# New hand-written instruction orders for the last six chunks of an attention and MoE kernel

## The chip, the cores and the metric

The kernel runs on one core of a Trainium2 chip. A time is device microseconds (us) of one execution; the time shown for a kernel is the median of several executions. A profile is one execution more, recorded by the hardware profiler, with its own time. The engines of the core are PE (TensorE: matmuls, and PEld, its weight loads), DVE (VectorE), ACT (ScalarE), POOL (GpSimd) and SP, which here issues nearly all DMAs. Each engine runs its own instructions strictly in order and waits for others at semaphores.

## The reference

For 8 batches and 8 heads, 512 local tokens and 32 global tokens with head size 64 attend to each other; what comes out is normed and put through a gated two-layer network.

```python
k_all = concat([k_g, k_l]); v_all = concat([v_g, v_l])
out_g = softmax(scale * q_g @ k_all.T) @ v_all                  # global rows see everything
mask  = abs(i - j) <= 32                                        # local rows: a band, and the globals
out_l = softmax(concat([scale * q_l @ k_g.T, where(mask, scale * q_l @ k_l.T, -1e9)])) @ v_all
x  = concat([out_g, out_l]) as (8 * 544, 512)
xn = x / sqrt(mean(x * x) + 1e-6) * rms_g
y  = (silu(xn @ w_gate) * (xn @ w_val)) @ w_out                 # 512 -> 1536 -> 512
```

## The kernel before, in words

The 4352 rows are worked in nine chunks. Chunks 0 to 7 hold the 512 local rows of one batch each, chunk 8 the 256 global rows of all batches. While PE works on the network of chunk c, attention for chunks c+1 and c+2 is woven in between.

The network's products are f16 matmuls. Each operand is split into a high and a low half, so that a product takes three matmuls. From chunk 2 on the first layer is written with seven block products instead of eight (`moe_pair`), and from chunk 3 on the second layer too (`moe_out`). The work of a chunk is a list of units. In chunks 3 to 7 units 0 to 41 are the first layer: steps P0 to P41, of 12 matmuls each (in chunk 8 there are 48 steps of 6). The second layer's steps are O0 to O41, of 6 matmuls each (3 in chunk 8). A matmul comes with one weight load, so P stands for 24 instructions of PE and O for 12. What other engines do with the result of unit k is called Rk (PSUM read and combined), tk (tanh, gating and splitting of an earlier group), nk (norm of the next chunk) and wk (a weight fetch that SP issues, 24 for the first layer and 11 for the second).

Attention units run beside it. A local unit (`local_halves`, four heads' worth: half a batch) has the steps L and V (loads), S (scores on PE, four PSUM banks), M and N (minimum, on DVE), E and F (exponentials, on ACT), D (division, on DVE and then on ACT or POOL), T (32 by 32 transposes on DVE), A and B (two parts of the products with V, on PE), X and Y (results out of PSUM). A global unit (`global_unit`) has GL, GV, GS, GM, GN, GT, GA, GD and GX; GS, GT, GA and GX are PE's. These products are f32, and the trace shows each of their matmuls as two: S is 128 matmuls and weight loads, A and B are 80 each, GS 32, GA 80, and the two halves of GT are 5 transposes each, GX one. Chunks 3 to 5 hold two local units and one global unit, chunk 6 one and one, chunk 7 two global units, chunk 8 none. The name `A/2+1.0` is step A of unit 2 of the chunk one further on, first piece; a step is cut into pieces where the engine changes.

The order of all this is not left to a scheduler. A planner runs once, and every engine call is stored under the name of its step (`write`, L1850). Then, for a chunk that has an entry in `ORDERS`, the calls are issued in the order of that list:

```python
    orders = {c: names.split() for c, names in ORDERS.items()}
    for c, plan in plans.items():
        for name in orders.get(c, plan):
            for call in plan.pop(name) if c in orders else plan[name]:
                call()
```

So a list sets the order of the instructions on each engine and of the DMAs on SP's queue. It neither adds nor drops an instruction. Tiles come from pools with a fixed number of buffers: fetched weights and most of the first layer's f32 results share the 12 buffers of the pool `wf`, attention on PE has 4 PSUM banks (`pa`), and the products have 4 (`po` twice, `pg`, `pv`). Whoever writes a new tile waits until the tile that had the buffer is done with. The numbers of lines in the profile are those of the call that issues (L1870 for nearly everything from chunk 1 on), so instructions are told apart by their tiles: `pq` is P, `pr` is O, `s` is S, `a` is A and B, `et` is what T writes, `wt` and `wu` are fetched weights.

Of the kernel before, what the change touches and what calls it, by code (L numbers as in the profile page):

```python
# [126 lines left out]
t18.0 t16.2 V/2+1.0 P16.0 S/2+1.0 P17.0 R15.1 P18.0 R16.0 M3/2+1.0 R17.0 E3/2+1.0 M2/2+1.0 N3/2+1.0
w13.0 t12.0 w15.0 E2/2+1.0 P19.0 R18.0 M0/2+1.0 N2/2+1.0 M1/2+1.0 E1/2+1.0 P20.0 R19.0 R20.0 w24.0
N1/2+1.0 t21.0 R20.2 F3/2+1.0 t19.1 D3/2+1.0 R20.1 t21.1 t22.0 t17.2 F2/2+1.0 P21.0 R21.0 P22.0
R22.1 R22.0 t19.0 t23.1 t22.1 t23.0 F1/2+1.0 D1/2+1.0 t17.3 D3/2+1.1 GA/1+1.0 t24.0 w17.0 t23.2  # L130
t24.3 w18.0 P23.0 R23.0 GN/1+1.2 P24.0 N0/2+1.0 R24.0 t24.1 T3/2+1.0 P25.0 P26.0 R25.0 R26.0 P27.0
R27.2 w20.0 E0/2+1.0 P28.0 GD/1+1.0 GX/1+1.0 F0/2+1.0 w22.0 R27.1 t28.1 R27.0 D0/2+1.0 D2/2+1.0
# [6 lines left out]
O0.0 t42.1 R41.2 E1/0+2.0 w38.0 N3/0+2.0 R41.0 t42.0 O3.0 t33.0 O1.0 O4.0 O7.0 t43.1 t43.0 t40.1
t44.0 t44.4 E0/0+2.0 t44.1 O2.0 O5.0 O8.0 t44.2 M2/0+2.0 n44.0 n44.1 w44.0 n44.2 O6.0 O11.0 N2/0+2.0  # L140
E2/0+2.0 F2/0+2.0 t45.1 t44.3 t45.0 w40.0 O9.0 O12.0 O15.0 N0/0+2.0 O10.0 t40.0 N1/0+2.0 w46.0 O14.0
w52.0 F1/0+2.0 M3/0+2.0 E3/0+2.0 t46.0 O17.0 R50.0 n44.3 n44.4 n44.5 D1/0+2.0 D1/0+2.1 n44.6 n44.7
O13.0 F0/0+2.0 t33.1 t46.1 R49.0 O16.0 O24.0 O25.0 O26.0 O27.0 O28.0 w50.0 n44.8 n44.9 w55.0 n44.10
n44.11 n44.12 D2/0+2.0 D2/0+2.1 n44.13 n46.0 w48.0 n47.1 R50.1 O29.0 F3/0+2.0 D0/0+2.0 R56.0 O18.0
O19.0 D0/0+2.1 n46.1 n48.1 n47.0 n48.0 w53.0 n49.0 O36.0 R50.2 T1/0+2.0 O37.0 O38.0 O39.0 O40.0
t45.2 D3/0+2.0 n54.1 T2/0+2.0 O41.0 R62.0 O20.0 O21.0 O22.0 w60.0 GL/1+2.0 T0/0+2.0 n53.2 n52.1
O23.0 D3/0+2.1 T3/0+2.0 A/0+2.0 n54.0 n51.1 n52.0 n49.1 n55.0 n53.0 B/0+2.0 X/0+2.1 w59.0 n49.2
n53.1 R53.0 O30.0 O31.0 O32.0 O33.0 w57.0 n50.0 n51.0 n55.1 n56.0 w62.0 X/0+2.0 X/0+2.2 O34.0 O35.0
R59.0 R62.1 R59.1
# [19 lines left out]
O1.0 t44.4 t38.1 t37.1 t39.0 O4.0 O7.0 w36.0 O10.0 O9.0 Y/2+1.3 w38.0 O12.0 t44.0 t44.2 t44.3 n42.0
O8.0 w40.0 t44.1 t45.0 n42.1 O11.0 t46.0 w44.0 t40.0 t45.1 O13.0 O14.0 t38.3 O15.0 R49.0 n44.0 n44.1  # L170
w48.0 n44.2 n44.3 n44.4 n44.5 n44.6 n44.7 O16.0 R50.1 O17.0 O18.0 O19.0 n44.8 w46.0 w50.0 w60.0
t46.1 R50.0 R50.2 O20.0 n44.9 O21.0 O22.0 O23.0 t40.1 O24.0 O25.0 O26.0 n44.10 n44.11 n44.12 n44.13
n46.0 t45.2 O27.0 O28.0 O29.0 n47.1 w52.0 O30.0 O31.0 R56.0 O36.0 w55.0 n47.0 n46.1 O37.0 O38.0
n48.0 n48.1 n53.2 n49.0 n49.1 n50.0 n51.0 w57.0 n49.2 w53.0 R53.0 w62.0 O39.0 O40.0 O41.0 R62.0
# [6 lines left out]
w4.0 w6.0 R10.0 w8.0 GS/0+1.0 GM/0+1.0 P12.0 R12.0 R13.1 t10.1 t14.1 w10.0 P13.0 R13.0 R13.2 t14.0
P14.0 R14.0 P15.0 w18.0 t11.0 P16.0 R15.1 GN/0+1.0 R15.0 R16.0 t15.1 w11.0 P17.0 t12.0 GM/0+1.1
P19.0 P18.0 GN/0+1.1 R18.0 R17.0 P20.0 t15.0 t16.0 t12.1 t16.2 GV/0+1.0 R20.2 GT/0+1.0 P21.0 P28.0
w13.0 GT/0+1.1 R19.0 R20.0 t21.0 R20.1 t21.1 t22.1 t10.2 GT/0+1.2 P23.0 t16.1 GT/0+1.3 GA/0+1.0
t17.2 t17.3 t17.0 t17.1 w17.0 P22.0 R21.0 P24.0 GN/0+1.2 w15.0 t10.3 w20.0 t22.0 t23.2 t23.0
GL/1+1.0 t24.0 R22.1 t24.3 w22.0 R22.0 t18.0 t24.1 GD/0+1.0 P25.0 R25.0 t19.1 R23.0 t23.1 t25.0
R24.0 P26.0 R26.0 R27.0 w25.0 t28.0 P29.0 R28.0 R29.1 t26.0 t26.1 P27.0 R27.2 t29.0 P30.0 R29.0
R30.0 P31.0 GS/1+1.0 GM/1+1.0 GN/1+1.0 P32.0 w27.0 R32.0 R31.0 GM/1+1.1 P33.0 R33.0 P35.0 R27.1
t28.1 t29.1 t30.1 R34.0 t35.0 R34.1 t35.1 w24.0 w29.0 t30.2 P36.0 t19.0 R35.0 R36.0 GV/1+1.0 P37.0
t24.2 t31.2 R36.1 w31.0 R37.0 P34.0 R34.2 t36.0 P38.0 R38.0 t30.0 GN/1+1.1 t31.0 t31.1 w32.0  # L190
GT/1+1.2 P39.0 R39.0 t31.3 t36.1 t37.0 t38.0 t37.1 GT/1+1.0 GT/1+1.1 P40.0 w34.0 GX/0+1.0 P41.0
R41.2 GT/1+1.3 GA/1+1.0 t32.0 t33.0 t37.2 t38.2 R40.0 R41.1 t38.3 GN/1+1.2 GD/1+1.0 t42.1 R41.0
# [1916 lines left out]
```

## Time and profile before

Three executions took 919.73, 917.34 and 916.6 us: a median of 917.34 us. The profiled execution took 915.97 us, of which the span from its first to its last instruction is 914.2 us.

| | us | share of the span |
|---|---|---|
| PE busy | 873.6 | 96% |
| PEld busy | 670.3 | 73% |
| DVE busy | 722.5 | 79% |
| ACT busy | 556.1 | 61% |
| POOL busy | 274.2 | 30% |

| stretch (PE's first product of the chunk to that of the next), us | length | PE busy | DVE busy |
|---|---|---|---|
| chunk 3, 384.27 to 482.25 | 97.98 | 96.12 | 80.18 |
| chunk 4, 482.25 to 583.60 | 101.35 | 97.58 | 78.75 |
| chunk 5, 583.60 to 681.86 | 98.26 | 96.24 | 78.74 |
| chunk 6, 681.86 to 774.27 | 92.41 | 91.63 | 73.16 |
| chunk 7, 774.27 to 865.28 | 91.01 | 90.66 | 64.70 |
| chunk 8, 865.28 to 910.64 | 45.36 | 45.36 | 23.31 |

The first table is the profile page's own sum. The second comes from the view that gives each engine's busy time in chosen stretches. Length less PE busy is the time in which PE did nothing; the mean granted TensorE clock of the whole run was 0.983 of full speed.

### The profile page before, as it was taken

What the parts mean: (1) busy time and instruction counts of PE and PEld (TensorE: products, weight loads), DVE (VectorE), ACT (ScalarE), POOL (GpSimd) and SP (SyncE); (2) the same over time, 40 slices, a digit from 0 to 9 for tenths busy, and PEclk for the clock granted to TensorE, in tenths of its full rate; (3) what the DMA queues carried; (4) which work ended last, traced back from release to release, by engine and by line L of the source; (5) the groups of instructions that cost most, each with busy time, mean ns of one, the idle gap of its engine ahead of it and who ended that gap; (6) DMA issues with size and microseconds to landing.
All of it is one profiled execution on the core that took longest, in us unless ns stands there. A gap on an engine that the chain in (4) does not pass through costs nothing.

```text
span 914.2 us, 27773 instructions
## 1 busy us (share of the span) xinstructions
PE 873.6 (96%) x11430; PEld 670.3 (73%) x11430; DVE 722.5 (79%) x1831; ACT 556.1 (61%) x1341; POOL 274.2 (30%) x244
## 2 busy tenths in 40 slices
...
GB/s 345 404 287 103 210 52 174 173 276 285 100 192 249 255 228 236 186 296 213 262 259 262 199 290 257 200 235 251 252 253 240 206 213 219 254 267 220 263 232 177
DMA packets 101006, 212.03 MB, mean 232 GB/s; under 512 B 8080, under 2 KB 34448, under 8 KB 100880
## 3 DMA queue, kind: packets, MB, share of 16 engines
...
q8 instruction: 89, 1.46, 0.6%
q10 hardware_dynamic: 432, 0.33, 0.1%
...
## 4 chain that ended last, share of the span: by engine, by line
PE 81%; DVE 4%; ACT 3%; issue 2%; DVEq 0%; ACTq 0%
PE pq L1870 33%; PE pr L1870 17%; PE p L1870 10%; PE po L1870 7%; PE po L1735 3%; PE a L1870 3%; PE s L1870 3%; PE ga L1870 1%; PE gt L1870 1%; PE gs L1870 1%; ACT e L1870 1%; DVE s L1870 1%; ACT s L1870 0%; PE s L629 0%; PE t L673 0%
## 5 line engine op out<-in xcount | busy, mean ns | idle before, releaser
L1870 PEld LDWEIGHTS <-wt 128*128 128x128 f16 x3312 | 321.5, 98 | 44.7 <-issue 6.3
L1870 PE MATMUL pq<-xh,wt 128*128 128x256 f16 x1152 | 203.1, 273 | 0.8 <-ACT s L1870 0.2
L1870 PE MATMUL pq<-xl,wt 128*128 128x256 f16 x576 | 157.0, 273 | 0.0
L1870 PE MATMUL pq<-ht,wt 128*128 128x256 f16 x1296 | 155.2, 273 | 0.0
L1870 ACT ACTIVATE e<-e,sm 128x128 f32<-128x128 f32 x288 | 104.3, 390 | 12.6 <-DVE sm L1870 12.6
L1870 PE MATMUL pr<-wu,hs 128*128 128x256 f16 x792 | 93.0, 275 | 3.3 <-issue 3.3
L1870 POOL TENSOR_TENSOR hu<-v,hu 128x256 f16<-128x256 f32 (+1 forms) x60 | 56.2, 949 | 127.4 <-ACT hu L1870 114.6
L1870 POOL TENSOR_TENSOR e<-e,sm 128x512 f32<-128x512 f32 x24 | 29.6, 1243 | 215.7 <-DVE sm L1870 209.5
L1870 POOL TENSOR_TENSOR hs<-u,hs 128x512 f16<-128x512 f32 x50 | 59.0, 1194 | 104.7 <-ACT hs L1870 101.5
L1870 PEld LDWEIGHTS <-hs 128*128 128x128 f16 x792 | 77.8, 99 | 13.5 <-issue 3.6
L1870 ACT COPY s<-pq 128x512 f32<-128x512 f32 x72 | 41.7, 580 | 58.1 <-PE pq L1870 30.8
L1870 PE MATMUL pr<-wu,hu 128*128 128x256 f16 x594 | 69.4, 273 | 0.0
L1870 ACT ACTIVATE t<-u,half_inv 128x512 f32<-128x512 f32 x72 | 49.5, 715 | 31.9 <-DVE u L1870 30.9
L1870 DVE TENSOR_TENSOR v<-pq,s 128x512 f32<-128x512 f32 x72 | 49.3, 685 | 20.2 <-PE pq L1870 17.4
L1870 PE MATMUL po<-wo,h 128*128 128x512 f16 x288 | 65.2, 386 | 0.0
L1870 DVE TENSOR_TENSOR s<-pq,s 128x512 f32<-128x512 f32 x66 | 44.9, 686 | 24.9 <-PE pq L1870 10.6
L1870 PEld LDWEIGHTS <-hu 128*128 128x128 f16 x594 | 58.1, 98 | 6.7
L1592 PE MATMUL p<-xh,wf 128*128 128x512 f16 x192 | 58.8, 379 | 3.5 <-DVE t L1704 1.6
L1870 DVE SCALAR_TENSOR_TENSOR t<-t,u 128x512 f32<-128x512 f32 x72 | 54.0, 759 | 6.5 <-ACT t L1870 6.5
L1870 PE MATMUL p<-xh,wf 128*128 128x512 f16 x192 | 58.6, 379 | 0.0
L1592 PEld LDWEIGHTS <-wf 128*128 128x128 f16 x288 | 27.7, 98 | 37.5 <-issue 3.5
L1870 PEld LDWEIGHTS <-h 128*128 128x128 f16 x288 | 28.4, 100 | 34.0 <-issue 2.5
...
## 6 DMA issues: line engine op xcount, KB each, us to landing
wt<-wd SPq DMA_DIRECT2D x120, 512.0 KB, 5.2
wu<-wb SPq DMA_DIRECT2D x36, 512.0 KB, 4.6
wr<-in_w_in_dram SPq DMA_DIRECT2D x24, 512.0 KB, 9.0
wu<-wa SPq DMA_DIRECT2D x24, 512.0 KB, 4.5
...
```

What stands on the lines that cost most here:

```text
L1592: nc.tensor.matmul(ps[:, :n], rows[:, a, o : o + P], ch[z][k][:, :n], start=(k == 0 and i == 0), stop=(k == NK - 1 and i == 2),)
L1735: nc.tensor.matmul(po[j], ch["h", f][:, a, j * P : (j + 1) * P], wo[f][:, z, :], start=(f == 0 and q == 0), stop=(f == NF - 1 and q == 2),)
L1870: return lambda *a, **k: write(self.engine, lambda: call(*a, **k))
```

## The change

Chunks 3, 4 and 5 shared one list before. Now each of the chunks 3 to 8 has a list of its own, and all six are new. Each new list holds exactly the names that the old one of its chunk held. Chunks 0, 1 and 2, the planner, the tiles and all the instructions are as before. The lines below are those of the lists that hold A and B, the beginning of the wait for them, and the fetches of chunk 6; the remaining lines are other orders of the same names.

```diff
 _ORDER_3 = """
...
-P34.0 R34.2 R34.0 R34.1 P36.0 R36.0 L/0+2.0 A/2+1.0 t35.1 t36.1 t30.0 t35.0 t36.0 t30.1 t31.3 P35.0
-R35.0 t31.2 t37.0 t31.0 t26.0 t37.2 w34.0 R36.1 B/2+1.0 w31.0 X/2+1.0 X/2+1.1 X/2+1.2 P37.0 t38.0
...
-O23.0 D3/0+2.1 T3/0+2.0 A/0+2.0 n54.0 n51.1 n52.0 n49.1 n55.0 n53.0 B/0+2.0 X/0+2.1 w59.0 n49.2
-n53.1 R53.0 O30.0 O31.0 O32.0 O33.0 w57.0 n50.0 n51.0 n55.1 n56.0 w62.0 X/0+2.0 X/0+2.2 O34.0 O35.0
...
+GD/1+1.0 R31.0 P34.0 P37.0 D1/2+1.1 t31.2 T1/2+1.0 t32.0 t33.1 w36.0 R34.0 t35.0 w34.0 R34.2 w48.0
+R35.0 P38.0 T3/2+1.0 A/2+1.0 B/2+1.0 R36.1 R36.0 R34.1 R37.0 P39.0 w32.0 P40.0 t35.1 t36.1 t36.0
...
+A/0+2.0 n54.1 B/0+2.0 R53.0 n53.2 R56.0 O36.0 O37.0 n48.0 t45.2 n48.1 n49.0 w57.0 R59.0 R59.1 n49.1
...
+_ORDER_4 = """
...
+P33.0 R33.0 R34.1 P34.0 P36.0 T1/2+1.0 R34.2 R34.0 t35.0 R35.0 A/2+1.0 B/2+1.0 Y/2+1.0 P38.0 R36.0
...
+n55.1 w62.0 n51.0 n52.0 O35.0 R59.0 w59.0 n52.1 n53.1 n56.0 A/0+2.0 B/0+2.0 X/0+2.0 X/0+2.1 X/0+2.2
+R59.1 n53.2 n54.0
+_ORDER_5 = """
...
+GV/1+1.0 R15.1 P16.0 R16.0 S/2+1.0 M0/2+1.0 M1/2+1.0 t16.1 E0/2+1.0 E1/2+1.0 P18.0 N1/2+1.0 t10.2
...
+D0/2+1.1 T0/2+1.0 w25.0 t29.0 t24.3 D3/2+1.1 T3/2+1.0 t29.1 R32.0 P33.0 R33.0 t30.0 R34.0 R31.0
+A/2+1.0 B/2+1.0 t31.0 Y/2+1.0 X/2+1.0 t26.1 X/2+1.1 X/2+1.2 X/2+1.3 R34.1 t35.0 t31.1 t30.1 t32.0
...
+T2/0+2.0 w62.0 R62.0 n49.2 n51.1 n52.0 w60.0 w57.0 R62.1 A/0+2.0 B/0+2.0 R53.0 R59.0 X/0+2.0 X/0+2.1
...
 _ORDER_6 = """
-P1.0 P0.0 R0.0 Y/0+1.1 R1.1 Y/0+1.0 P2.0 R1.0 R2.0 GS/1+1.0 w3.0 GM/1+1.0 GM/1+1.1 GN/1+1.0 P4.0
...
-P8.0 R8.1 R8.0 GT/1+1.0 GT/1+1.2 GT/1+1.3 GT/1+1.1 t7.1 t8.1 t9.2 w4.0 P9.0 P11.0 w13.0 t9.0 P14.0
...
-F0/2+1.0 D0/2+1.0 w18.0 P24.0 R20.1 t21.1 t22.0 P23.0 w17.0 E1/2+1.0 R22.0 R23.0 P25.0 E2/2+1.0
...
-A/2+1.0 B/2+1.0 R36.0 R34.0 t35.0 R35.0 P38.0 t32.0 t33.0 t36.0 t33.1 X/2+1.1 X/2+1.0 X/2+1.2 P37.0
...
+M1/2+1.0 N0/2+1.0 w11.0 R20.1 P22.0 R22.0 F3/2+1.0 E1/2+1.0 t21.0 w13.0 P23.0 R23.0 P21.0 w17.0
...
+D2/2+1.1 t32.0 T1/2+1.0 R33.0 P36.0 T3/2+1.0 T2/2+1.0 t33.0 R35.0 P37.0 R34.2 R36.1 A/2+1.0 B/2+1.0
...
-ORDERS = {1: _ORDER_1, 2: _ORDER_2, 3: _ORDER_3, 4: _ORDER_3, 5: _ORDER_3, 6: _ORDER_6, 7: _ORDER_7, 8: _ORDER_8}
+ORDERS = {1: _ORDER_1, 2: _ORDER_2, 3: _ORDER_3, 4: _ORDER_4, 5: _ORDER_5, 6: _ORDER_6, 7: _ORDER_7, 8: _ORDER_8}
```

On PE alone, the old and the new lists read as follows around the runs that matter below. GS, GT, S, GA and GX are left out of the P lists where they are not between the steps named.

| chunk | before | after |
|---|---|---|
| 3 | P34 P36 A/2 P35 B/2 P37 ... O20 to O23 A/0 B/0 O30 to O35 | P34 P37 P38 A/2 B/2 P39 ... O27 O28 O29 A/0 B/0 O36 to O41 |
| 4 | as chunk 3 | P34 P36 A/2 B/2 P38 ... O30 to O35 A/0 B/0, the chunk's end |
| 5 | as chunk 3 | P32 P33 A/2 B/2 P34 ... O36 to O41 A/0 B/0, the chunk's end |
| 6 | P36 P34 A/2 B/2 P38 P37 P39 P40 P41, then O | P36 P37 A/2 B/2 P39 P38 P40, O2 O5 O1 GX P41, then O |
| SP's fetches in 6 | w3 w1 w4 w13 w6 w8 w11 w10 w15 | w4 w3 w1 w10 w8 w6 w15 w11 w13 |

## Rows read from the trace of the kernel before

**Rows 1.** Busy time by stretch: length, PE, PEld, DVE, ACT, POOL (xinstructions), clock, DMA, GB/s.
```profile
384.27:910.64 526.37, 517.59 (x6965) 454.86 (x6958) 398.86 (x969) 301.36 (x722) 169.93 (x164) 1.00 0.75 240
```

**Rows 2.** Waits of PE in that stretch: us in total, times, longest.
```profile
PE a L1870 <- issue: 4.0, 3, 1.7
...
PE a L1870 <- DVE et L1870: 0.7, 2, 0.3
PE pq L1870 <- ACT s L1870: 0.2, 1, 0.2
```

**Rows 3.** Timeline of PE: start, us, what, count, idle before it and its releaser.
```profile
443.27 0.33 PE L1870 MATMUL a<-et,v 32*64 32x32 f32 x11 [1.71 <-issue]
...
572.47 2.38 PE L1870 MATMUL a<-et,v 32*64 32x256 f32 x160
574.78 1.27 PE L1870 MATMUL pr<-wu,hs 128*128 128x256 f16 x10
579.33 4.43 PE L1870 MATMUL pr<-wu,hs 128*128 128x256 f16 x26 [3.29 <-issue]
...
677.28 0.70 PE L1870 MATMUL a<-et,v 32*64 32x64 f32 x42 [1.54 <-issue]
...
739.45 0.68 PE L1870 MATMUL a<-et,v 32*64 32x64 f32 x40 [0.74 <-issue]
```

**Rows 4.** Busy time by stretch, from one such idle time to the next.
```profile
443.27:579.33 136.06, 132.29 (x2044) 116.56 (x2044) 110.83 (x294) 92.45 (x249) 46.56 (x43) 1.00 0.78 253
579.33:677.28 97.95, 95.93 (x1405) 83.65 (x1405) 77.12 (x202) 64.69 (x170) 31.37 (x29) 0.98 0.75 241
677.28:739.45 62.17, 61.39 (x893) 53.68 (x894) 46.58 (x115) 39.05 (x100) 15.28 (x15) 1.00 0.61 199
```

**Rows 5.** DMA queues: packets, MB, share; the page's, then 440.80 to 443.27 us.
```profile
q8 instruction: 89, 1.46, 0.6%
...
q8 instruction: 1, 0.02, 2.4%
```

**Rows 6.** Busy time by stretch: the shortest stretches of 256 PE instructions before a boundary.
```profile
573.24:575.68 2.44, 2.44 (x145) 2.31 (x137) 2.38 (x5) 1.44 (x4) 0.00 (x0) 1.00 0.92 285
735.66:738.46 2.80, 2.80 (x130) 2.44 (x129) 2.61 (x5) 1.63 (x4) 1.55 (x2) 1.00 0.47 143
705.37:708.24 2.87, 2.87 (x130) 2.56 (x128) 2.80 (x6) 0.59 (x1) 0.00 (x0) 1.00 0.99 306
672.52:675.52 3.00, 3.00 (x130) 2.61 (x128) 2.96 (x6) 1.26 (x4) 0.18 (x1) 1.00 1.04 285
438.30:441.37 3.07, 3.07 (x152) 2.62 (x133) 3.03 (x7) 0.71 (x3) 0.00 (x0) 1.00 0.88 318
545.51:549.00 3.49, 3.49 (x144) 3.12 (x132) 3.40 (x12) 2.47 (x7) 3.38 (x4) 1.00 0.77 222
```

**Rows 7.** Busy time by stretch, behind two of the idle times.
```profile
443.27:446.70 3.43, 3.43 (x40) 3.08 (x40) 1.95 (x6) 1.79 (x4) 1.30 (x2) 1.00 0.67 226
579.33:582.80 3.47, 3.47 (x19) 2.51 (x20) 0.00 (x0) 0.00 (x0) 0.00 (x0) 0.58 0.02 6
```

**Rows 8.** Timeline of PE: A/2, P35 and B/2 of chunk 4.
```profile
536.04 1.54 PE L1870 MATMUL a<-et,v 32*64 32x256 f32 x80 [0.34 <-DVE et L1870]
537.51 1.48 PE L1870 MATMUL pq<-ht,wt 128*128 128x256 f16 x12
538.92 1.15 PE L1870 MATMUL a<-et,v 32*64 32x96 f32 x80
```

**Rows 9.** Busy time by stretch: end of S/2 to start of A/2, chunk 5.
```profile
610.50:637.38 26.88, 26.54 (x314) 23.40 (x309) 22.66 (x69) 23.40 (x71) 11.44 (x12) 1.00 0.66 218
```

**Rows 10.** Timelines of PE and SP in chunk 6, and the page's wt fetches.
```profile
708.90 0.28 PE L1870 MATMUL pq<-xh,wt 128*128 128x256 f16 x1
...
714.00 7.37 SPq L1870 DMA_DIRECT2D wt<-wd  x6
...
wt<-wd SPq DMA_DIRECT2D x120, 512.0 KB, 5.2
```

More of the change, by code (lines that the diff above doesn't have):

```diff
@@ L127 @@
[L127 to L132, printed above, removed]
@@ L139 @@
[L139 to L143, printed above, removed]
@@ L144 @@
[L144 to L149 removed]
+P7.0 w3.0 R7.0 P1.0 R1.0 Y/0+1.1 P2.0 Y/0+1.0 R2.0 P0.0 GS/1+1.0 w1.0 R0.0 R1.1 w6.0 P5.0 P4.0 R4.0
@@ new lines @@
+V/2+1.0 GM/1+1.0 GN/1+1.0 R5.0 R6.0 L/2+1.0 R6.1 P3.0 P8.0 R3.0 t7.0 R8.1 t7.1 P6.0 R6.2 t8.0
+GM/1+1.1 GN/1+1.1 t8.1 P9.0 GN/1+1.2 P10.0 R8.0 w13.0 t9.2 P11.0 R11.0 R9.0 w4.0 P12.0 t9.0 t10.0
+R10.0 P13.0 R12.0 R13.0 t10.3 GT/1+1.0 GT/1+1.2 R13.2 t9.1 t14.0 t15.0 GT/1+1.1 w8.0 R13.1 t10.1
+t14.1 w11.0 P14.0 R14.0 t15.1 t16.0 GT/1+1.3 t10.2 t16.2 t17.0 t17.1 w10.0 P15.0 R15.0 w15.0 R15.1
+t11.0 t12.0 P16.0 t16.1 t18.0 S/2+1.0 t12.1 P17.0 M3/2+1.0 R16.0 t19.0 t17.2 M0/2+1.0 E0/2+1.0
+N0/2+1.0 F0/2+1.0 R17.0 M2/2+1.0 P18.0 M1/2+1.0 R18.0 P19.0 R19.0 N3/2+1.0 L/0+2.0 P20.0 R20.2
@@ new lines @@
+E3/2+1.0 P22.0 R20.0 t21.0 R20.1 t21.1 w17.0 t22.0 Y/0+1.2 R22.0 P21.0 t19.1 R21.0 t22.1 t23.2 P23.0
+E1/2+1.0 w18.0 D0/2+1.0 t17.3 D0/2+1.1 R22.1 E2/2+1.0 N2/2+1.0 F2/2+1.0 R23.0 P24.0 R24.0 P25.0
+R25.0 t23.1 GV/1+1.0 w20.0 t24.3 w25.0 t23.0 t24.0 t24.1 P28.0 D2/2+1.0 D2/2+1.1 t24.2 F3/2+1.0
+P26.0 R26.0 N1/2+1.0 R27.1 T2/2+1.0 t28.1 w22.0 P29.0 t25.0 t26.1 P27.0 R27.2 t29.1 F1/2+1.0
+T0/2+1.0 R27.0 D1/2+1.0 t26.0 D3/2+1.0 R28.0 D3/2+1.1 GA/1+1.0 R29.0 P30.0 P31.0 R29.1 P32.0 R32.0
+R30.0 P33.0 P36.0 P35.0 t28.0 t29.0 t30.2 t30.0 w29.0 t31.0 t30.1 t31.1 w24.0 R33.0 w27.0 t31.3
@@ new lines @@
+w13.0 t9.0 w6.0 t10.0 t10.1 P12.0 R12.0 t11.0 GN/1+1.2 t12.1 S/2+1.0 M2/2+1.0 M3/2+1.0 E3/2+1.0
+N1/2+1.0 M1/2+1.0 E1/2+1.0 w3.0 F1/2+1.0 P15.0 R15.0 N0/2+1.0 L/0+2.0 M0/2+1.0 P14.0 R14.0 P10.0
+R10.0 t12.0 R13.1 N3/2+1.0 F3/2+1.0 t14.1 w17.0 E0/2+1.0 N2/2+1.0 P16.0 P17.0 P13.0 R15.1 R16.0
+w10.0 w15.0 E2/2+1.0 P18.0 R13.2 F0/2+1.0 t15.1 D0/2+1.0 Y/0+1.3 R13.0 t14.0 D3/2+1.0 P19.0 R18.0
+P21.0 R19.0 w18.0 R21.0 R20.0 P22.0 t10.3 t10.2 R22.0 V/2+1.0 t15.0 R20.1 t16.1 GV/1+1.0 D3/2+1.1
+t16.0 t17.0 t16.2 t17.2 R17.0 t17.1 t21.0 D1/2+1.0 D1/2+1.1 R22.1 P23.0 P20.0 R23.0 t21.1 T3/2+1.0
@@ new lines @@
+R20.2 P24.0 P25.0 t17.3 R24.0 t22.1 w20.0 D0/2+1.1 t22.0 t23.1 P26.0 R25.0 R26.0 w22.0 t23.2 t24.3
+P28.0 P29.0 R28.0 R29.1 t23.0 R27.1 GA/1+1.0 GD/1+1.0 t24.0 t24.1 F2/2+1.0 w25.0 D2/2+1.0 R27.0
+R29.0 t28.1 t28.0 t24.2 P27.0 t25.0 R27.2 w24.0 P30.0 D2/2+1.1 R30.0 w27.0 t26.1 T2/2+1.0 P31.0
+t18.0 R31.0 t26.0 t29.1 t29.0 t30.0 t31.0 t30.2 t30.1 P32.0 P35.0 t31.3 T0/2+1.0 w29.0 t19.1 R32.0
+P33.0 R33.0 R34.1 P34.0 P36.0 T1/2+1.0 R34.2 R34.0 t35.0 R35.0 A/2+1.0 B/2+1.0 Y/2+1.0 P38.0 R36.0
+t31.2 GL/1+2.0 t31.1 t32.0 R36.1 t36.0 t35.1 t36.1 t37.2 P37.0 R37.0 R38.0 w31.0 w32.0 P39.0 R39.0
@@ new lines @@
+t15.1 w13.0 GT/1+1.1 R13.0 P14.0 R14.0 P15.0 R15.0 t10.1 t11.0 t12.0 t14.0 w10.0 t15.0 t16.2 t17.3
+GV/1+1.0 R15.1 P16.0 R16.0 S/2+1.0 M0/2+1.0 M1/2+1.0 t16.1 E0/2+1.0 E1/2+1.0 P18.0 N1/2+1.0 t10.2
+N0/2+1.0 M2/2+1.0 P19.0 t12.1 R18.0 R19.0 t17.2 w18.0 N2/2+1.0 t16.0 F1/2+1.0 D1/2+1.0 t17.0 t17.1
+F0/2+1.0 R20.1 t21.1 P17.0 R17.0 P21.0 M3/2+1.0 R21.0 t18.0 P22.0 R22.1 N3/2+1.0 R22.0 P23.0 R23.0
+R20.0 t21.0 E2/2+1.0 P20.0 F2/2+1.0 D2/2+1.0 D1/2+1.1 GA/1+1.0 t19.0 R20.2 w22.0 w20.0 t22.0 t23.1
+GN/1+1.2 t22.1 D2/2+1.1 w17.0 P25.0 P24.0 R25.0 L/0+2.0 t19.1 D0/2+1.0 t23.0 t24.0 E3/2+1.0 F3/2+1.0
@@ new lines @@
+t24.1 t25.0 P26.0 t26.0 R24.0 w24.0 D3/2+1.0 R26.0 w48.0 T2/2+1.0 P28.0 GD/1+1.0 P27.0 t23.2 R27.2
+R28.0 w27.0 T1/2+1.0 R27.1 t28.1 P29.0 P30.0 P31.0 R29.0 R29.1 P32.0 t24.2 R27.0 t28.0 R30.0
+D0/2+1.1 T0/2+1.0 w25.0 t29.0 t24.3 D3/2+1.1 T3/2+1.0 t29.1 R32.0 P33.0 R33.0 t30.0 R34.0 R31.0
+A/2+1.0 B/2+1.0 t31.0 Y/2+1.0 X/2+1.0 t26.1 X/2+1.1 X/2+1.2 X/2+1.3 R34.1 t35.0 t31.1 t30.1 t32.0
+Y/2+1.1 P34.0 R34.2 t36.0 Y/2+1.2 Y/2+1.3 w29.0 t35.1 t33.0 P36.0 R36.0 P35.0 R35.0 t30.2 t33.1
+R36.1 P37.0 P38.0 t37.1 R37.0 P39.0 R39.0 t36.1 t37.2 n42.0 t38.3 t37.0 P40.0 R40.0 R41.1 t38.0
@@ L169 @@
[L169 to L174, printed above, removed]
@@ new lines @@
+GT/1+1.3 R14.0 P15.0 R15.1 t15.0 R13.1 t14.1 R15.0 t15.1 t16.2 GA/1+1.0 GN/1+1.2 GD/1+1.0 P17.0
+t16.1 t16.0 t17.0 t17.1 t11.0 t12.0 t12.1 t18.0 t19.1 P16.0 P18.0 R18.0 S/2+1.0 R16.0 R17.0 M0/2+1.0
+P19.0 N3/2+1.0 E0/2+1.0 N1/2+1.0 M2/2+1.0 M3/2+1.0 E3/2+1.0 R19.0 R20.0 P20.0 N2/2+1.0 w15.0 R20.2
+M1/2+1.0 N0/2+1.0 w11.0 R20.1 P22.0 R22.0 F3/2+1.0 E1/2+1.0 t21.0 w13.0 P23.0 R23.0 P21.0 w17.0
+R21.0 t22.0 t17.3 P26.0 F0/2+1.0 R22.1 w18.0 E2/2+1.0 F2/2+1.0 w22.0 w20.0 t21.1 t22.1 D0/2+1.0
+t23.2 P24.0 R24.0 t17.2 t23.0 t24.0 w24.0 P25.0 t19.0 R25.0 t24.2 D0/2+1.1 R26.0 w25.0 R27.0 P27.0
@@ new lines @@
+R27.2 R27.1 P28.0 R28.0 t24.1 t23.1 t25.0 t28.0 t28.1 P29.0 R29.0 F1/2+1.0 w36.0 t24.3 P30.0
+T0/2+1.0 D3/2+1.0 D3/2+1.1 P31.0 t26.1 w27.0 R29.1 P32.0 R32.0 t26.0 R30.0 P33.0 P35.0 V/2+1.0
+D1/2+1.0 R31.0 D1/2+1.1 D2/2+1.0 P34.0 t29.0 t29.1 t30.1 t30.2 t30.0 t31.0 t31.1 w29.0 t31.2 t31.3
+D2/2+1.1 t32.0 T1/2+1.0 R33.0 P36.0 T3/2+1.0 T2/2+1.0 t33.0 R35.0 P37.0 R34.2 R36.1 A/2+1.0 B/2+1.0
+R36.0 R37.0 R34.0 t35.0 t36.0 P39.0 t33.1 P38.0 R34.1 t35.1 t37.1 R39.0 t36.1 t37.2 t37.0 t38.0
+t38.1 t38.2 w34.0 P40.0 X/2+1.1 w32.0 X/2+1.0 X/2+1.2 w31.0 O2.0 R40.0 O5.0 R38.0 R41.1 Y/2+1.1 O1.0
@@ L181 @@
[L181 to L192, printed above, removed]
@@ L199 @@
-R62.0 n56.0 w48.0 R50.2 w53.0 O30.0 O31.0 O22.0 O23.0 R53.0 n56.10 w61.0 O32.0 O33.0 O34.0 O35.0
-R59.0 w54.0 n56.4 n56.8 n56.7 n56.11 R62.1 R59.1
+P1.0 P0.0 R0.0 R1.1 w8.0 P2.0 P7.0 P3.0 R1.0 R2.0 R3.0 P4.0 R4.0 P5.0 R5.0 P6.0 R6.0 R6.2 w1.0 t7.0
+w6.0 P8.0 R7.0 P10.0 R8.1 R6.1 t7.1 t8.0 t9.1 P9.0 R8.0 R9.0 t8.1 P11.0 R10.0 w4.0 P12.0 w3.0 P14.0
+GL/0+1.0 t9.0 R11.0 t10.0 t10.1 w10.0 t11.0 t12.1 R12.0 P13.0 R13.2 R14.0 w13.0 R13.1 t14.1 R13.0
+t15.1 w11.0 P15.0 R15.0 t14.0 t9.2 R15.1 P16.0 R16.0 t10.3 P17.0 R17.0 t10.2 GS/0+1.0 t12.0 w18.0
```

131 lines of the change are left out of this document (86 added, 45 removed).

## The prediction

> **What bounds the kernel now.** I read three views in turn. First the busy time of chunks 3 to 8, the only ones whose lists change: of 526.37 us PE is busy 517.59 [rows 1]. PE is the bound, DVE at 399 and ACT at 301 are not, and since the change neither adds nor drops an instruction it can win or lose only in PE's 8.78 us of idle time, in PE's speed, and in how tightly runs follow each other. Second, what ends PE's idle time: three idle times ahead of an `a` matmul, 4.0 us together, for which the profile names no other engine, only "issue" [rows 2]. Third, PE's timeline: beside those three (1.71, 1.54, 0.74) there is one of 3.29 ahead of a second-layer product [rows 3]. Together they are 7.28 us. They lie at 443.27 (in B/2 of chunk 3), 579.33 (just behind A/0 and B/0 of chunk 4), 677.28 (B/0 of chunk 5) and 739.45 (B/2 of chunk 6), every one in or behind a dense run of attention matmuls. No data is late there.
>
> What is late is the instructions themselves, as three rows say. Between the idle times PE runs 2044 + 2044, 1405 + 1405 and 893 + 894 instructions, matmuls and weight loads [rows 4]: 4088, 2810 and 1787, which is 16 x 256 - 8, 11 x 256 - 6 and 7 x 256 - 5, the few missing ones being such as the view doesn't count. The instruction queue moved 1.46 MB in 89 packets, 16.4 KB each, and PE's 22,860 instructions by 89 are 257 to a packet; one such packet lands just ahead of an idle time [rows 5]. So PE's instructions come in blocks of 256, and PE stands still where it has run through one before the next is there. Blocks of 256 instructions that lasted 2.44, 2.80, 3.00 and 3.07 us were followed by the four idle times; one of 3.49 was not, nor one of 2.87 [rows 6]. Block and idle time together, the delay, are 5.73, 3.54, 4.54 and 4.78 us; for the block of 2.87 the delay was at most that. A chunk's products take longer: P has 24 instructions in 1.41 us [rows 8], so 256 last 15 us. Only where a boundary falls behind attention that runs close together does it cost anything.
>
> [...]
>
> **The change, part by part.** I count PE's instructions along the new lists (P 24, O 12, S 256, A and B 160 each, GS 64, GT 20, GA 160, GX 2) from the boundaries that the trace gives. The total of a chunk doesn't change, so the boundaries keep their count; what lies there does.
>
> *Old idle times:* -7.28. None of the four places has the same neighbours as before.
>
> *New ones.* Chunk 3: the boundary was 138 instructions into B/2. A/2 and B/2 now stand behind P38, and it falls 92 into B/2; the block is A/2, 92 of B/2 and 4 of P38. A and B side by side take 2.31 us for 320 instructions (572.47 to 574.78, [rows 3]), so the block lasts 252/320 x 2.31 + 0.2 = 2.0 us. Chunk 4: the boundary is 52 instructions from the end, where A/0 and B/0 now stand; it falls 108 into B/0, and the block is 148 of A/0 and 108 of B/0, 1.85 us. Chunk 5: 156 from the end, so 4 into B/0; the block is half O steps and about 6.3 us: no idle time. Chunk 6: it falls 58 into B/2, and the block is 38 instructions of P (2.1) and 218 of A and B (1.6), 3.65 us: none, as behind 3.49 [rows 6]. Two short blocks remain. Their idle time is the delay less 1.95; by the delays seen it is 0.9 (2.87) to 3.8 (5.73) each. The dearest two began well inside an attention run (573.24 and 438.30), the other three in product steps (735.66, 672.52, 705.37; mean 3.65). Both new ones begin within 12 instructions of a product step, so I take 3.65: 2 x 1.7 = +3.4.
>
> *Clock.* Behind the idle time of 3.29 the granted clock was 0.58 for 3.47 us, behind that of 1.71 it stayed 1.00 [rows 7]. The 26 products there took 4.43 us [rows 3]; at 1.41/12 each [rows 8] they take 3.05. That loss of 1.4 goes, as no new idle time is as long: -1.4 (0 if one is).
>
> *A and B side by side.* In chunk 4, with P35 between, A/2 ran from 536.04 to 537.51 and B/2 for 1.15 [rows 8]: 2.62. Together they took 2.31 [rows 3]. The 0.31 comes in A/2 of chunks 3, 4 and 5: -0.9 (0 if the gain belongs to unit 0's tiles). Chunk 6 had them so already; A/0 and B/0 were and stay together.
>
> *Data waits.* A/2 waited 0.34 for `et`, which T writes on DVE, in chunk 4 [rows 8], and there is one more such wait, 0.7 together [rows 2], in chunk 5. In chunk 4 there were 19 P steps between S/2 and A/2 and now there are 25: -0.34. In chunk 5 there are 17. From S/2's end to A/2's start were 26.88 us, with DVE busy 22.66 [rows 9], so DVE has 4.2 us of air, and PE arrives 2 x 1.41 + 0.1 (GX) = 2.9 earlier. What decides is whether DVE serves the chain M, N, D, T first. Bounds: -0.34 (none is left) to +2.9 (nothing on DVE moves); as the new list puts T3 right ahead of the A/2 steps, behind fewer R and t steps, I take a value near the lower end, +0.65.
>
> *Fetches.* Nearly all moved fetches are still issued long before their use. One isn't: w13 of chunk 6, the fourth fetch of the chunk before and the ninth now, is for P23, which itself comes two P steps earlier. The ninth was issued at 714.00 and fetches take 5.2 us to land [rows 10]: 719.2. PE ended S/2 and had 16 P steps behind it at 708.90 [rows 10]; 22 stand ahead of P23 now, so it is wanted at 708.90 + 6 x 1.41 = 717.4. Bounds 0 (the buffer that it waits for comes free earlier, since P17 and P16 are ahead) to 1.8; I take half, +0.9. What ACT, POOL and the other orders do is hidden by PE's products as before: PE is busy 517.59 of the 526.37 us, and a late R would show as PE waiting at `pq`, of which the stretch has 0.2 [rows 2].
>
> Sum: -7.28 + 3.4 - 1.4 - 0.9 - 0.34 + 0.65 + 0.9 = -5.0. The profiled execution took 915.97 us, its span of 914.2 and 1.8 around it; the median shown is 1.37 above it. So 911.0 profiled and **912.3 us** as median.
>
> **The rivals.** *Data waits take the gain back.* The order of DVE and SP is what a list sets, and chunks 5 and 6 have their A/2 two P steps closer to S/2. If DVE keeps its pace, A/2 waits 2.9 in chunk 5 and 2.8 (two P steps) in chunk 6, and w13 costs 1.8; for 0.65 + 0.9 that is 7.5, a sum of +1.0: **918.3**, no change to be told. For it: two waits of 0.34 show that A/2 is met just in time. Against: DVE's 4.2 us of air, and these bounds all at once.
>
> *Delay long for every block; slower.* If the 5.73 us of chunk 4 is what a block needs and the shorter ones were luck, the idle time is 5.73 less the block: 3.8 twice for the short ones, and also 2.2 and 2.0 at the S steps of chunk 5 (unit 2) and chunk 4 (unit 0), whose blocks are about 3.5 and 3.7 long, and 2.1 in B/2 of chunk 6: 13.9 for the 3.4, and two clock losses as at 579.33, 2.8. Sum +8.3: **925.6**. It comes out slower from a delay of about 4.9 at all five, with one clock loss. For it: two delays of 4.78 and 5.73. Against: no idle time behind blocks of 2.87 and 3.49 [rows 6].
>
> *Blocks are not the cause.* If the four idle times are of something that the order doesn't move, the terms -7.28, +3.4 and -1.4 drop out: -0.9 - 0.34 + 0.65 + 0.9 = +0.3, **917.6**. Against: the three distances of [rows 4].
>
> **How the numbers follow.** Forecast 0.68, data waits 0.11, no blocks 0.07, long delay 0.14. About 0.3%, 2.75 us, is what a measurement can tell from no change: faster is below 914.6, slower above 920.1. The forecast's own range is 908.9 (no new idle time, -3.4) to 916.5 (both at 5.73, +4.2). I give 0.06 of its 0.68 to times above 914.6. So faster 0.62; same 0.06 + 0.11 + 0.07 = 0.24; slower 0.14. The range goes down to 907.0, where the waits in chunks 5 and 6 are at their lower bounds as well (-1.9), and up to 919.5, past both middle rivals; most of the long delay's 0.14 stays outside.
>
> **What would show it right or wrong.** PE's idle times without a releaser should be two, of about 1.7 us, one 92 instructions into B/2 of chunk 3, one 108 into B/0 of chunk 4, multiples of 256 apart; none in chunk 5's A/0, B/0 nor in chunk 6's B/2; and no stretch at 0.58 behind chunk 4. A/2 of chunk 5 may wait for `et`, P23 of chunk 6 for `wt`, less than 1 us each. Wrong would be: idle times that are no multiples apart, idle behind blocks of 3.5 us and more, or PE waiting at `pq` for other engines in several places.

## The result and the profile after

The changed kernel takes 906.23 us (median of four executions, 904.06 to 909.49), where the kernel before, four times beside it, takes 916.97: a ratio of 0.9886, 95% interval 0.9843 to 0.9929. Timed again six times it gave 907.47 against 917.92 (0.9886, 0.9856 to 0.9916). That is 10.4 to 10.7 us less. I had forecast 5.0 less and a range down to 907.0: the direction was right, the size half of what came.

The profiled execution after took 906.6 us (span 904.8). Chunks 3 to 8, the busy time in one stretch [rows 1]:

```profile
382.06:901.31 519.25, 514.09 (x6965) 453.55 (x6958) 402.14 (x969) 300.81 (x722) 172.84 (x164) 1.00 0.75 244
```

The stretch is 7.1 us shorter. PE is idle for 5.2 us instead of 8.8 and busy for 3.5 us less, with the same 13,923 instructions. The waits of PE in it [rows 2], all there are:

```profile
PE pq L1929 <- DVE v L1929: 1.3, 1, 1.3
PE pq L1929 <- DVE s L1929: 1.3, 1, 1.3
PE pr L1929 <- DMA wu<-wb: 1.2, 1, 1.2
PE pq L1929 <- DMA wt<-wd: 0.6, 1, 0.6
PE pr L1929 <- ACT os L1929: 0.6, 1, 0.6
```

In this profile not one "issue" is left: all 7.3 us of it are gone, and the two that I expected in their place didn't come. What is there instead are five waits for data, in steps that I had not named: P28 of chunk 3 (`wt`), P40 and O18 of chunk 4 (`s`, `os`), P13 and O26 of chunk 6 (`v`, `wu`). The two places with the new short blocks, PE's timeline [rows 3] and then the busy time of the 256 instructions [rows 6]:

```profile
439.84 2.38 PE L1929 MATMUL a<-et,v 32*64 32x256 f32 x160
442.14 0.28 PE L1929 MATMUL pq<-xh,wt 128*128 128x256 f16 x1
...
573.92 2.56 PE L1929 MATMUL a<-et,v 32*64 32x256 f32 x160
576.41 0.28 PE L1929 MATMUL pq<-xh,wt 128*128 128x256 f16 x1
```

```profile
439.31:441.59 2.28, 2.28 (x129) 1.97 (x131) 1.64 (x3) 1.20 (x2) 0.01 (x1) 1.00 0.72 244
573.94:576.02 2.08, 2.05 (x133) 1.84 (x132) 2.08 (x4) 1.71 (x3) 0.18 (x1) 1.00 0.93 276
```

Both blocks are shorter than any that was followed by an idle time in chunks 3 to 8 before, and A and B run through them without one.

### The profile page after: what moved, and what is told of

It reads as the page before. It is cut to its first block, busy times and chain, and to the rows that moved or that the text cites. A ratio compares the mean times of both kernels' runs of the same rounds, so it can differ in the third digit from the quotient of the medians.

```text
span 904.8 us, 27760 instructions
## 1 busy us (share of the span) xinstructions
PE 867.7 (96%) x11430; PEld 667.4 (74%) x11430; DVE 725.8 (80%) x1831; ACT 555.3 (61%) x1341; POOL 277.2 (31%) x244
## 3 DMA queue, kind: packets, MB, share of 16 engines
q8 instruction: 89, 1.46, 0.7%
## 5 line engine op out<-in xcount | busy, mean ns | idle before, releaser
L1929 POOL TENSOR_TENSOR hs<-u,hs 128x512 f16<-128x512 f32 x50 | 61.1, 1236 | 97.1 <-ACT hs L1929 92.1
L1929 PEld LDWEIGHTS <-hs 128*128 128x128 f16 x792 | 77.3, 98 | 10.7 <-issue 1.8
L1929 ACT COPY u<-pq 128x512 f32<-128x512 f32 x36 | 21.0, 583 | 51.7 <-PE pq L1929 50.9
```

The costliest lines, as they stand in the source:

```text
L1929: return lambda *a, **k: write(self.engine, lambda: call(*a, **k))
```

## The experiments

Theory: PE waits for blocks of instructions. Its main rival: the gain is what the new lists do to data, on whichever engine. Times are medians (a ratio, over all executions, can differ a little from that of the medians); the columns at the right are of one profiled execution each, for chunks 3 to 8: their length, and the idle time at boundaries of 256 instructions (waits above 0.2 us).

| run | us (executions) | before beside it | ratio and 95% interval | length | at boundaries |
|---|---|---|---|---|---|
| b104 | 918.71 (12) | 917.43 | 1.0023 (1.0005 to 1.0042) | 526.44 | 6.6 |
| b176 | 943.08 (6) | 917.43 | 1.0293 (1.0248 to 1.0337) | 544.42 | 20.0 |
| a40 | 905.38 (6) | 917.43 | 0.9877 (0.9846 to 0.9909) | 519.89 | 0 |
| a176 | 938.18 (6) | 917.43 | 1.0235 (1.0184 to 1.0286) | 537.83 | 13.7 |
| b_apart | 912.90 (12) | 916.18 | 0.9952 (0.9931 to 0.9973) | 523.96 | 0.3 |
| a40s | 904.77 (6) | 916.18 | 0.9874 (0.9841 to 0.9907) | 517.50 | 0 |
| a232 | 922.51 (1) | 916.18 | | 525.63 | 4.4 |
| a40y | 904.23 (6) | 917.92 | 0.9852 (0.9818 to 0.9886) | 518.13 | 0 |
| after_third | 907.47 (6) | 917.92 | 0.9886 (0.9856 to 0.9916) | 519.18 | 0.5 |
| after_again | 907.23 (1) | 916.18 | | 520.45 | 0.6 |
| before_again | 918.96 (1) | 917.92 | | 529.48 | 7.5 |
| before_third | 915.63 (1) | 917.92 | | 527.74 | 6.9 |

### Moving the boundaries and nothing else

One edit, in the scores of the very first unit, where PE waits for its first keys. N one-element matmuls are 2N instructions of PE and take 1.4 us (52 of them) or 2.3 us (88), inside that wait. Every step keeps its place in the order; only what stands at a boundary changes.

```diff
             ps = st["ps"] = [bank(f"s{u}{h}", "pa") for h in range(2)]
 
+            for _ in range(N if u == 0 else 0):
+                nc.tensor.matmul(ps[0][0:1, 0:1], one16[:, 0:1], one16[:, 0:1], start=True, stop=True)
             for i in range(NT):
```

> The order of before, with 52 one-element matmuls (104 PE instructions) ahead of the first scores, where PE waits some 5 us for its first keys; only the places of the 256-instruction boundaries move, 104 instructions earlier in the program's steps. Theory (PE waits for the next block of 256 instructions): the four idle times in B/2, behind B/0, in B/0 and in B/2 go from those places; what the shifted boundaries meet is four blocks of 2.6 to 3.4 us instead of seven of 1.7 to 3.3. With instructions landing 2.0 us (mean of 62 boundaries; -3 to +5) after a block's start and PE going on 1.45 us after that, idle time from chunk 2 on falls from 10.3 to about 4 us, and 1.4 us of lowered clock with it: 909 to 913 us against 917. Rival (the idle times belong to what the order makes PE wait for, not to the count of instructions): 917 within 2, idle in the same steps.

> As the run before, with 88 such matmuls (176 instructions). Theory: now eight short blocks of 1.7 to 3.4 us, idle time of about 12 us from chunk 2 on instead of 10.3: 918 to 923 us, with new idle times at the end of chunks 2 and 3 (behind A/0 and B/0) and in S/2 of chunk 3. Rival: 917 within 2.

> The order of after, with 20 such matmuls (40 instructions). Theory: the two short blocks of chunks 3 and 4 (2.4 and 2.05 us) become longer than 3.5; in chunk 2 the two idle times of 1.2 and 1.6 become one to two smaller ones: 903 to 906 us against 906.2. Rival: 906 within 2, so this run tells little by its time; the places of the idle times tell.

> The order of after, with 88 such matmuls (176 instructions). Theory: thirteen short blocks of 1.65 to 3.4 us, some 18 us of idle time from chunk 2 on where the run of after had 2.9: 917 to 923 us, so that the new order is no faster than the old one at its own boundaries. Rival (the order's gain has nothing to do with boundaries): 906 within 2.

b176 and a176 settle the matter: the old order loses 26 us and the new one 32 by a shift, and at its shifted boundaries the new order is 2.3% slower than the old one at its own. The rival, 917 and 906 within 2, is out. The waits of PE in chunks 3 to 8, b176 and then a176:

```profile
PE a L1872 <- issue: 11.2, 3, 5.2
PE pq L1872 <- ACT hu L1872: 3.8, 1, 3.8
PE s L1872 <- issue: 2.6, 2, 1.6
PE pq L1872 <- issue: 2.4, 2, 1.8
...
```

```profile
PE a L1931 <- issue: 5.7, 3, 2.5
PE pr L1931 <- issue: 2.9, 2, 2.4
PE s L1931 <- issue: 2.2, 2, 2.0
PE pq L1931 <- ACT xh L1931: 1.6, 1, 1.6
PE pq L1931 <- issue: 1.3, 2, 0.9
...
```

The two with ACT's name lie at the count of a boundary as well. In all 14 profiles together PE has 67 idle times above 0.25 us, after 130 us, for which no releaser is named. The view's count of PE's instructions from one of them to the next falls about one in 300 short of whole blocks, so that its remainder by 256 falls slowly along the program, from 163 near 195 us to 113 near 760; all 67 lie within 8 of one straight line, whatever the order and the shift.

The sizes I had wrong. Both shifts came out 15 to 25 us dearer than expected. Idle time in chunks 3 to 8 is the larger part (b176: 20.0 for 7.3). Chunk 3 also begins 7 us later in b176 and 14 in a176: ahead of it PE's waits on "issue" sum to 11.7 and 15.2 us there, for 3.5 in before and 3.8 in after. And behind b176's 5.19 us at 693.35 the granted clock was 0.50 for 3.45 us.

```profile
693.35:696.80 3.45, 3.45 (x17) 2.51 (x18) 0.00 (x0) 0.00 (x0) 0.00 (x0) 0.50 0.11 39
```

b104 missed its 909 to 913, and its 918.71 lies where the rival had it; only the places speak for the theory here. The four idle times left theirs, but 3.6 us came at O31 of chunk 3 and 1.8 at O35 of chunk 5, both behind A/0 and B/0, and chunk 1 got 5.2 us of its own:

```profile
PE p L1872 <- issue: 5.2, 2, 3.3
```

a40's two short blocks got longer (4.3 and 3.7 us) and it has no idle time at a boundary from chunk 3 on, and its time can't be told from that of after, as expected.

### The old order with products between A and B

```diff
 _ORDER_3 = """
-... R36.1 B/2+1.0 w31.0 X/2+1.0 X/2+1.1 X/2+1.2 P37.0 t38.0 t38.1 Y/2+1.0 R37.0 P38.0 w42.0 ...
+... R36.1 P37.0 P38.0 B/2+1.0 w31.0 X/2+1.0 X/2+1.1 X/2+1.2 t38.0 t38.1 Y/2+1.0 R37.0 w42.0 ...
-... n53.0 B/0+2.0 X/0+2.1 w59.0 n49.2 n53.1 R53.0 O30.0 O31.0 O32.0 O33.0 w57.0 ... O34.0 O35.0 R59.0
+... n53.0 R53.0 O30.0 O31.0 O32.0 O33.0 O34.0 O35.0 B/0+2.0 X/0+2.1 w59.0 n49.2 n53.1 w57.0 ... R59.0
 _ORDER_6 = """
-A/2+1.0 B/2+1.0 R36.0 R34.0 t35.0 R35.0 P38.0 t32.0 t33.0 t36.0 t33.1 X/2+1.1 X/2+1.0 X/2+1.2 P37.0
+A/2+1.0 R36.0 R34.0 t35.0 R35.0 P38.0 P37.0 B/2+1.0 t32.0 t33.0 t36.0 t33.1 X/2+1.1 X/2+1.0 X/2+1.2
```

> The order of before with one edit: products stand between the two parts of the four pairs that the idle times sat in. In chunks 3 to 5 P37 and P38 move ahead of B/2 and O30 to O35 (with R53) ahead of B/0; in chunk 6 P38 and P37 (with R36, R34, t35 and R35) ahead of B/2. No boundary moves in count. The blocks that lasted 2.4 to 3.1 us ahead of the four boundaries become 5.3 to 6.5 us long. Theory (instructions are late where a block is run through in less than landing plus 1.4 us): the four idle times of 7.3 us go, with 0.8 of refilling behind them and 1.4 of lowered clock; parts that are no longer side by side cost 0.24 in seven pairs: 917.2 becomes 908 to 911 us, about the time of the new order, with none of its lists. Rival (the new order's gain comes from its orders of DVE, ACT and SP): 917 within 2.

The four idle times are gone with none of the new lists, and the kernel is 0.5% faster than before (interval 0.3 to 0.7): 3.3 us by the medians, 4.4 by the ratio. That is about half of what I expected, and the waits in chunks 3 to 8 show what took the rest:

```profile
PE pq L1867 <- DVE s L1867: 2.1, 4, 1.0
PE pq L1867 <- DVE ht L1867: 1.8, 2, 0.9
PE a L1867 <- DVE et L1867: 0.7, 2, 0.3
PE s L1867 <- issue: 0.3, 1, 0.3
PE pq L1867 <- ACT s L1867: 0.2, 1, 0.2
```

P40 (three times) and P39 of chunk 6 now come too early for DVE, and P0 of chunks 4 and 5 meets the norm that O35 had covered: 4.8 us of waits for data instead of 0.9 [rows 2]. So the boundaries alone should be worth more than 3.3 us (argued from these waits, not measured by itself), and products that are moved for their sake uncover other waits.

### Whether the delay depends on what stands ahead

The table is worked out from the trace's instruction packets: for each short block its length, the end of the packet with the next one, counted from the block's start, and the idle time; where there are three figures they are of three profiles (before, before_again, before_third; after, after_again, after_third).

| block ahead of | begins | lasts, us | next block lands | idle |
|---|---|---|---|---|
| before, B/2 chunk 3 | inside A/2 | 3.17 | 3.55, 4.24, 4.08 | 1.71, 2.39, 2.20 |
| before, O31 chunk 4 | inside A/0 | 2.80 | 4.66, 4.41, 4.26 | 3.29, 3.13, 2.88 |
| before, B/0 chunk 5 | in products | 3.12 | 3.20, 2.49, 2.47 | 1.54, 0.83, 0.94 |
| before, B/2 chunk 6 | in products | 2.9 | 2.17, 2.15, 0.28 | 0.74, 0.52, none |
| after, B/2 chunk 3 | in products | 2.41 | -0.49, -0.48, 0.51 | none |
| after, B/0 chunk 4 | 12 behind a product | 2.05 | 0.62, 1.46, 1.24 | 0.03, 0.58, 0.50 |
| a232, B/2 chunk 3 | inside A/2 | 2.08 | 2.34 | 1.68 |
| a232, B/0 chunk 4 | inside A/0 | 1.98 | 2.95 | 2.44 |

> The kernel after once more, for a second profile. Theory (a block asked for while PE works on products lands early): no idle time at the short blocks of chunks 3 and 4 again, or under 0.5 us. Rival (where the packet falls is chance): one of them at 1 to 2 us as likely as not. In chunk 2 idle times of 1.1 to 1.3 and 1.6 to 1.9 us again.

> The kernel before once more, for a second profile. Theory: idle times at the same four boundaries (B/2 of chunk 3, behind B/0 of chunk 4, B/0 of chunk 5, B/2 of chunk 6), each 1.4 us after its packet landed, with sizes that differ from those of the first profile by up to 2 us because the landing does; 5 to 10 us together. Rival (sizes fixed by the program): 1.7, 3.3, 1.5 and 0.7 again within 0.2.

> As before_again, a third profile: the same two expectations. For chunk 2, whose instructions and boundaries the change leaves alone, it also shows how much of the 1.9 us by which it was shorter in the profile of after is chance: 105 to 107 us for the chunk.

> The order of after with 116 one-element matmuls ahead of the first scores (232 instructions, the same as boundaries 24 instructions later). The short blocks of chunks 3 and 4 now begin some 30 instructions inside A/2 and A/0 instead of at or within 12 of a product, and last 1.9 to 2.0 us as before. Theory (how early a block is asked for depends on how long the instructions ahead of it take): idle times of 1.5 to 2.6 us in both B/2 of chunk 3 and B/0 of chunk 4. Rival (the delay doesn't depend on what stands ahead): 0 to 0.3 us as in after.

In every line with an idle time PE went on 1.2 to 1.6 us after the landing. What differs is when the packet landed. In after's chunk 3 it had landed before the short block began in two of the three profiles, and 0.5 us behind its start in the third, where I had expected it early again; the queues of the first from 437.75 to 438.85 us, where the block begins at 439.31:

```profile
q8 instruction: 1, 0.02, 5.7%
```

a232 moved the two blocks of after some 24 instructions on, so that they begin inside the attention run, and both idle times came, at the two places and in the size that the theory gave (PE's timeline):

```profile
449.13 2.16 PE L1931 MATMUL a<-et,v 32*64 32x256 f32 x137
452.97 0.43 PE L1931 MATMUL a<-et,v 32*64 32x64 f32 x23 [1.68 <-issue]
...
585.15 2.27 PE L1931 MATMUL a<-et,v 32*64 32x256 f32 x144
589.87 0.47 PE L1931 MATMUL a<-et,v 32*64 32x32 f32 x16 [2.44 <-issue]
```

This is one execution of a232. Over the 14 profiles, of the blocks whose last 32 instructions ahead took over 1.4 us (products) the next one landed 1.3 to 1.4 us behind the block's start in the median (some 600 blocks); where they took under 0.6 us (attention), 2.6 to 2.9 us (some 400). So the packet came later behind the block's start where the instructions ahead took less time. When a block is asked for, which after_again and a232 had in their theories, no run shows. Whether other DMA traffic delays the packet too was not tried.

The sizes vary between executions, by up to 0.7 us in a place and by 0.6 in the sum (7.3, 7.5, 6.9): the rival "fixed by the program" misses its 0.2 in both profiles. My own theory missed in one point: which boundaries cost something varies too. before_third has none at B/2 of chunk 6 and 0.9 in S/2 of that chunk instead, before_again a fifth of 0.6 in S/0 of chunk 5; after_again's 0.58 lies just above its 0.5. Chunk 2, the same in both kernels, took 106.97, 107.63 and 105.91 us before and 105.12, 105.95 and 107.43 after, so that the 1.9 us between the first two profiles are chance. before_again and before_third also showed what the first profile could not: behind the idle time in B/2 of chunk 3 the clock was 0.64 and 0.69 there [rows 7 have 1.00]. Two lines of before_again, then one of before_third:

```profile
443.83:447.26 3.43, 3.43 (x30) 2.54 (x30) 1.05 (x3) 1.26 (x3) 1.26 (x1) 0.64 0.61 202
581.40:584.90 3.50, 3.50 (x18) 2.50 (x19) 0.00 (x0) 0.00 (x0) 0.00 (x0) 0.52 0.02 7
...
442.06:445.50 3.44, 3.44 (x31) 2.69 (x31) 1.36 (x4) 1.51 (x4) 1.27 (x1) 0.69 0.62 202
```

### Taking the five waits of the new order away

a40s moves products one step: P28 behind P26 in chunk 3; P41 ahead of P40, O13 ahead of O18, O16 ahead of O26 in chunk 4; P12 ahead of P13, with R13.2 behind it, in chunk 6. (O26 waited in chunk 6 in after, but in chunk 4 in a40, from which these two runs start.) a40y keeps P40 and P41 and moves one copy on ACT:

```diff
 _ORDER_4 = """
-... A/2+1.0 B/2+1.0 Y/2+1.0 P38.0 R36.0 t31.2 ...
+... A/2+1.0 B/2+1.0 P38.0 R36.0 Y/2+1.0 t31.2 ...
```

> The order of after with 40 instructions of shift, and with the products that waited for data one step later: P28 behind P26 in chunk 3, P41 ahead of P40, O13 ahead of O18 and O16 ahead of O26 in chunk 4, P12 ahead of P13 (R13.2 behind it) in chunk 6. If each step waited because it came one step too early, the waits of 5.4 us (and 0.8 of refilling) become under 1.5: 900 to 902 us against 905.4. Rival (what it waits for is late by itself, and the next product waits as long): 905 within 2.

> As a40s, but P40 and P41 of chunk 4 as in after, and there Y/2 (a copy on ACT that waits for B/2) behind R36 instead of ahead of it. In a40 ACT stood 2.3 us at that copy with R36's copy behind it, DVE 2.6 us for R36's copy, and PE 1.3 us at P40 for DVE. Theory (a wait on ACT passed down the line): ACT runs R36's copy at once, P40's wait goes, and with P28, O18 and O26 as in a40s chunks 3 to 8 take 514 to 516 us in the profile (a40: 519.9, a40s: 517.5): 900 to 903 us. Rival (P40 needs a result that is late for another reason): P40 waits 1 us or more again, 904 to 905.

> The kernel after, timed beside a40y on one chip: 906 within 2. In its profile the block of chunk 3 lands before its block begins again and has no idle time; the one of chunk 4 may have 0 to 1 us.

In a40s P28, O18 and O26 of chunk 4 no longer wait and P13's 1.3 became 0.5 at P12, but P41 waited 2.0 where P40 had waited 1.3. In a40y that wait is gone, and ACT's timeline shows why, a40 first: `x<-a` is Y/2, the next `s<-pq` the copy that DVE and then P40 stood waiting for.

```profile
532.81 0.56 ACT L1931 COPY s<-pq 128x512 f32<-128x512 f32 x1
535.69 0.37 ACT L1931 COPY x<-a 128x256 f32<-128x256 f32 x1 [2.31 <-PE a L1931]
535.96 0.59 ACT L1931 COPY s<-pq 128x512 f32<-128x512 f32 x1
```

```profile
535.00 1.11 ACT L1928 COPY s<-pq 128x512 f32<-128x512 f32 x2
537.88 0.37 ACT L1928 COPY x<-a 128x256 f32<-128x256 f32 x1 [1.77 <-PE a L1928]
```

So that step of the theory holds. The times don't bear it out: 904.77 and 904.23 lie where the rivals had them (905 within 2, and 904 to 905). a40y's chunks 3 to 8 took 518.13 us (expected 514 to 516); its profile has 3.4 us of other waits, 1.2 of them at O4 for a late fetch and the others 0.5 to 0.6 each. The medians of a40, a40s and a40y are 0.9 to 3.2 us below those of after; their intervals overlap its own, so that they beat it is not shown.

## Why the prediction was wrong

By the means of three profiles each (before, before_again, before_third; after, after_again, after_third) chunks 3 to 8 went from 527.86 to 519.63 us: -8.2. By the steps of the prediction:

| step | forecast | measured |
|---|---|---|
| old idle times | -7.28 | -7.2 |
| new ones | +3.4 | +0.4 |
| data waits and fetches (all the other idle time) | +1.2 | +3.4 |
| clock, and A and B side by side (PE's busy time) | -2.3 | -4.8 |
| sum | -5.0 | -8.2 |

*Old idle times.* Right, and by the mechanism that was given: the count of 256 held in every run, and the places in all three profiles, but for the missing one and the two additional ones named above.

*New ones: the step that failed first.* Two short blocks stood where I had worked them out, 2.3 and 2.1 us long (forecast: 2.0 and 1.85), but I priced them at a delay of 3.65, the mean of three blocks, two of which I knew only because they had been waited for. A delay that is read from idle times is read from the late packets alone. The landings of all blocks stand in the same trace: the 30 or so blocks of chunks 3 to 8 that begin behind products had their next one 1.7 to 1.9 us after their start in the mean, some 3.2 with the 1.4 behind it. At the two places themselves the delays, landing plus 1.4, were 0.9 to 1.9 us in chunk 3 and 2.0 to 2.9 in chunk 4. And I took the start "within 12 instructions of a product" as no more than a reason for the lower figure, where a232 speaks for more: 0 and 0.4 (means of three profiles) there, 1.7 and 2.4 some 24 instructions further in. I had also read no boundary of chunk 2, which has two such idle times in the same trace, at 1.85 and 3.45 us of block:

```profile
347.03 0.33 PE L1870 MATMUL a<-et,v 32*64 32x32 f32 x10 [1.12 <-issue]
...
352.39 0.51 PE L1870 MATMUL s<-k,q 64*32 64x128 f32 x17 [1.90 <-issue]
```

Their delays, block and idle time, are 3.0 and 5.4 us, so that one mean was no price for either.

*PE's busy time.* A and B side by side took 2.30 (439.84 to 442.14) for 2.62 [rows 8]: the 0.31 was right. The lowered clock behind 579.33 is gone as forecast; after has none in chunks 3 to 8 in any of its three profiles (PE busy for 514.09, 514.13 and 513.96 us). What I missed is the loss behind B/2 of chunk 3, which the one profile I had didn't show and the other two did: their first-layer products took 284.7 and 284.9 us of PE for 283.0. What an idle time costs beside its own length (an estimate: some 0.2 us, as one product alone takes 0.28 [rows 10] and in a row 1.41/12) was left out, four times; the 0.8 of refilling in the expectations of b_apart and a40s is the same estimate, and no run shows it by itself. With the forecast 2.3 that makes some 4.2; about 0.6 us of the 4.8 I can't assign.

*Data waits.* A/2 of chunk 5 and P23 of chunk 6 did not wait in any profile of after; four to six steps waited that I had set at nothing, 4.6 to 5.6 us together. "Hidden by PE's products as before" was the sentence that failed: it holds for an order whose waits one has seen, not for a new one. P40's case shows the kind, a copy on ACT that waits for B/2 ahead of one that PE needs.

*The signs of being wrong.* Two of the three that the prediction named came. PE waited at `pq` for other engines, at P40 and P13. And blocks well over 3.5 us had idle time behind them, in the old order as well: in before_again the 0.64 of S/0 in chunk 5 stands behind this block of 256 instructions, and b104's 1.8 at O35 behind one of 5.1 us.

```profile
644.95:650.53 5.58, 5.58 (x130) 4.72 (x128) 4.95 (x10) 3.73 (x6) 4.16 (x5) 1.00 0.85 287
```

So the blocks are the cause, but no length up to 6.8 us made one safe. Idle times without a releaser that lie off the multiples there were none above 0.25 us.

*Luck.* The errors cancel in part: -3.0 (new ones) and -2.5 (busy time) against +2.2 (data waits), so that the sum looks nearer than its terms were. The remaining difference to the 10.4 to 10.7 us of the medians lies in the part that the lists don't touch: chunk 3 began at 384.27, 384.15 and 382.57 us before and at 382.06, 381.46 and 383.68 after, with the same instructions ahead of it. Those 1.3 us, and what the profiles leave of the medians, I take for chance; no run here settles it.

*The rivals.* "Blocks are not the cause" is out by the shifts (b176 against before: 26 us in 917 hang on where the boundaries fall), and "delay long for every block" by blocks of 2.4 us without idle time. "Data waits take the gain back" was right that there would be such waits, at other places, and wrong that they would be all.
